# Talking-heads attention with two mixtures of experts: how the attention stage starts, loads and hands over

## The chip, the cores and the metric
One core of one Trainium2 chip runs the whole program. The metric is the time of the program on the device in microseconds (us). Three runs of the kernel before took 1065.91, 1069.70 and 1069.84 us; their median, 1069.7 us, is the time before.

## What is computed
All data is fp32. Attention has 4 batches, 12 heads, 448 positions and a head width of 64; its scores are mixed over the heads before the softmax and again after it ("talking heads"). Its result, 1792 rows of 768, goes through two layers of 8 experts with one expert per row:

```python
scores = einsum('bhij,hg->bgij', scale * q @ kT, w_pre)
attn   = softmax(scores, axis=-1)
attn   = einsum('bhij,hg->bgij', attn, w_post)
x      = (attn @ v) as 1792 x 768
# layer 1: e = argmax(cosine(x, expert_emb)); x = gate * relu(x @ w1[e]) @ w2[e]
# layer 2: only rows with x @ w_skip > 0:     x += gate * relu(x @ w1[e]) @ w2[e]
```

## The kernel before
**Attention** is cut into 16 units (u = 0 to 15; batch u // 4, a quarter m = u % 4 of its positions: 120 rows, or 88 for m = 3). The heads of a unit are taken in six pairs. `qk` (L310) computes the scores of one pair on TensorE; ScalarE, or for the first six pairs ScalarE and VectorE, copies them from PSUM to one of three `stage` buffers; `put` (L293) moves them by two DMAs on SyncE's queue into `sraw[u % 2]`, where heads and rows are interleaved on the 128 partitions, so that one matmul can mix the heads. A unit then has 6 steps (5 for m = 3). In a step `pre` (L334) mixes 120 rows, `top` and `ex` (VectorE, ScalarE) are the softmax, `post` (L378) mixes and turns the result with 128 small matmuls, and `out_t` copies it to `at`: one half by ScalarE (L406), one by VectorE (L408). The main loop (L1144) writes the order by hand: in step k it issues `pre(k + 2)`, `post(k)`, up to two `qk` pairs (a plan, L1140, gives "q" for a pair and "r" for a `rows_job`), and one `av` (L410), the product with v of the unit before. `av` writes the one PSUM bank with tag "D"; ScalarE alone empties it (L427), and it does so before the next `av` can begin.

What lies beside this main work waits in a list, `side`; `mu(n)` runs its next n entries, some ten a step. Among them is the routing of a finished unit: `rows_job` (L527) puts its rows back in order, writes them to `x_d` in DRAM (L588), finds each row's expert on VectorE (some 35 short operations one after the other), counts the row's place in that expert's list with a matmul (`rank`, L468) and scatters row number and gate to a table in DRAM (L490). `cum[1]` holds how many rows each expert has so far.

**The queues.** SyncE's queue carries the puts and, later, the expert weights. GpSimd's queue, which works strictly in order and has eight DMA semaphores in turn, carries q (`load_q`, three buffers), k (`load_k`, two buffers; k of a batch is one tile of 6 head pairs, loaded by two DMAs of 672 KB), v (`load_v`), the zeros and the tables.

**The start** (L1078 to L1107): q of unit 0 on SyncE's queue, k of batch 0 on ScalarE's queue in two parts, mixing weights and q on GpSimd's. Partitions 12, 25, 38, 51 and 77, 90, 103, 116 of `sraw` belong to no head, but `pre` multiplies them by zero weights, so they must hold finite numbers. Four DMAs on GpSimd's queue (L1092) copy zeros there, each to 4 partitions, 84 KB, before six `qk` pairs are run ahead.

**Other zeros.** `zero_fill` (L222) clears `y_d`, which the first layer scatters to: seven DMAs of 768 KB, one in step t = 3 of the units 1 to 7. Zeros also go to the last 89 rows of `x_d` (L217).

**The hand-over to the experts.** The first tile of 128 rows of expert 0 (`early`, L1116) is gathered from `x_d` by the table's first 128 places. It is closed by `pad_steps` (L605): a matmul counts the rows, and `cum[1]` is raised to 128 if there are fewer, so that later rows go to later places. This follows the routing of unit 14 (L546). At step `prefetch_at` (L1113; step t = 4 of unit 14), q, k and `stage` are given up for weights, and the first two of the weight chunks (128 x 1536 each) are loaded. Each chunk is split into a high and a low part: ScalarE rounds it (L723), and the rest is a subtraction (L728). `split_pieces` (L734) does this for the first four chunks in thirds, three thirds a step in the last unit, with the subtraction on GpSimd. After the loop (L1208 to L1217) the rest of `side` is run, and then the six `av` of unit 15; the buffers of attention are freed, the rows of unit 15 are computed (`rows_steps`, L551, L564), the first tile is turned (`t_T`, L775) and its first expert matmul follows (L781). The second tile of expert 0 needs the routing of unit 15: a read of the table (`entries`, 1024 entries), then a gather (L1238 and L1239).

Of the kernel before, what the change touches and what calls it, by code (L numbers as in the profile page):

```python
# [32 lines left out]
def talking_heads_moe_moe(tc, A, out):  # L33
# [177 lines left out]
    def setup_tables():  # L211
# [4 lines left out]
        st = [  # L216
            lambda: nc.gpsimd.dma_start(x_d[NTOK - 88:], z[:89]),  # L217
# [4 lines left out]
        fill = lambda r: nc.gpsimd.dma_start(yz[:, 2 * r:2 * r + 2], z.unsqueeze(1).to_broadcast([128, 2, DM]))  # L222
        return st, fill, z
# [54 lines left out]
    def load_k(b, lo=0, hi=6, eng=None):  # L278
        if lo == 0:
            ks[b] = aR.tile([128, 6, S], F32, tag="k", name="k", bufs=2)  # L280
        for g in range(2):
            (eng or nc.gpsimd).dma_start(
                ks[b][64 * g:64 * g + 64, lo:hi], A["kT"][b].rearrange("d (p g) j -> d g p j", g=2)[:, g, lo:hi]
            )
# [25 lines left out]
    def qk(u, pr, both=False, eng=None):  # L310
# [8 lines left out]
        for x in range(2):  # L319
            nc.tensor.matmul(p[x] if both else p[:, x], qs[u][64 * x:64 * x + 64, pr, :n], ks[b][64 * x:64 * x + 64, pr])  # L320
# [89 lines left out]
    def av(u, pr):  # L410
# [5 lines left out]
        p = psum("D", "av")[:, :10 * ng]  # L416
# [9 lines left out]
        def copy(o, i):  # L426
            nc.scalar.activation(o, i, AF.Copy)  # L427
# [99 lines left out]
    def rows_job(u, early):  # L527
# [8 lines left out]
        def evac():  # L536
# [9 lines left out]
            if u == NU - 2:  # L546
                side.extend([lazy(pad_steps), early])
# [57 lines left out]
    def pad_steps():  # L605
# [6 lines left out]
        def count():  # L612
            busy["D"] = True
            box["p"] = psum("D", "count")[:, :8]
            nc.tensor.matmul(box["p"], C["ones"], cum[1])
# [3 lines left out]
            lambda: free(v.tensor_scalar(pad[w], box["p"][w], -1.0, 128.0, op0=ALU.mult, op1=ALU.add)),  # L619
            lambda: v.tensor_scalar(pad[w], pad[w], 0.0, 1.0 / 32.0, op0=ALU.max, op1=ALU.mult),  # L620
            lambda: v.tensor_tensor(cum[1][w], cum[1][w], pad[w], op=ALU.add),
# [126 lines left out]
    def entry(tabi, row):  # L748
        ent = P["wL"].tile([128, 2], U32, tag="ent", name="ent", bufs=4)
# [327 lines left out]
    with ctx, tc.manual_schedule():  # L1077
        load_q(0, nc.sync)  # L1078
        load_k(0, 0, 2, nc.scalar)
        st, zero_fill, z = setup_tables()  # L1080
# [3 lines left out]
        ps["now"], ps["D"] = psA, 1  # L1084
        load_k(0, 2, 6, nc.scalar)
# [13 lines left out]
        load_q(2)  # L1099
# [26 lines left out]
        def pair():  # L1126
# [17 lines left out]
        for k in range(NT):  # L1144
# [3 lines left out]
            if u == 0:  # L1148
# [3 lines left out]
                if t == 3:  # L1152
                    load_q(3)
                if t == 5:
                    load_k(1)
            if u == NU - 1:
                plan = ("r" if t in (2, 3) else "", "")

            def job(x):
                if x == "q":  # L1160
                    pair()
                elif x == "r":
                    v = u - 2 if t == 2 else u - 1
# [22 lines left out]
            if u > 0:  # L1186
                n = 2 if u == NU - 1 else 1
# [10 lines left out]
                if t == 3 and u <= 7:  # L1198
# [6 lines left out]
            if k > prefetch_at:  # L1205
                for _ in range(3):
                    next(pieces, None)
        flush("dve")  # L1208
        flush("act")
        for f in state.pop("spare"):  # L1210
            f(psum("D", "rank"))
        while side:
            mu()
        last = rows_steps(NU - 1, 0)
        for p in range(6):
            av(NU - 1, p)
            flush("dve")  # L1217
# [190 lines left out]
```

## Time and profile before

| what | value |
|---|---|
| median of 3 runs | 1069.7 us |
| the profiled execution's own time | 1069.07 us |
| its span, first to last instruction | 1067.4 us |
| TensorE busy | 950.1 us, 89% of the span |
| VectorE busy | 685.1 us, 64% |
| ScalarE busy | 612.4 us, 57% |
| GpSimd busy | 316.8 us, 30% |
| DMA moved | 211.19 MB, 198 GB/s on average |
| mean granted clock of TensorE | 0.947 of full speed |

The span leaves 1.67 us of the execution's time outside it. A share of busy time is a mean over stages: up to some 500 us attention runs, then the first expert layer, then from some 850 us the second. PE is TensorE, PEld its weight loads, DVE VectorE, ACT ScalarE, POOL GpSimd, SPq SyncE's queue. "idle before <-X" names what ended the idle time ahead of an instruction; "issue" means that the profile shows no wait. L numbers are lines of the kernel.

### The profile page before, as it was taken

To read this page: it belongs to the slowest core of one execution; us is meant where nothing else is said; L and a number is where in the kernel's file an instruction comes from. 1 tells how busy PE (TensorE), PEld (TensorE's weight loads), DVE (VectorE), ACT (ScalarE), POOL (GpSimd) and SP (SyncE) were. 2 spreads that over 40 slices of the span, in tenths; PEclk is the share of its full clock that TensorE was granted. 3 is DMA by queue.
4 is the path that set the end of the run, shared out by engine and by line. 5 is a ranking of instruction groups with operands and counts; after the bars stand their busy time and mean duration, and the time that the engine had idled before them with its cause. 6 is when DMAs were issued, how large, how long until landed. Compare 5 with 4: busy or idle time off the path is not lost. (4 is left out here: it accounts for less than half of the span.)

```text
span 1067.4 us, 29848 instructions
## 1 busy us (share of the span) xinstructions
PE 950.1 (89%) x12292; PEld 752.3 (70%) x12292; DVE 685.1 (64%) x1897; ACT 612.4 (57%) x1123; POOL 316.8 (30%) x326
## 2 busy tenths in 40 slices
PE   3087979998999999985889999999999997999996
PEld 1034545565556655654679999999999986889895
DVE  1064646775677757765357666666666586889995
ACT  1064747775777778764355444444444455777773
POOL 5522201521142114024253123233232233153422
PEclk9588979998999999998689999999999998999999
DMA  8748446746564446333459866477566677899960
GB/s 113 152 129 213 115 147 169 189 146 188 160 170 112 128 137 145 108 118 115 150 222 409 315 207 207 164 237 228 176 220 209 203 261 267 307 366 385 379 233 15
DMA packets 67008, 211.19 MB, mean 198 GB/s; under 512 B 14580, under 2 KB 37745, under 8 KB 66864
## 3 DMA queue, kind: packets, MB, share of 16 engines
q1 hardware_dynamic: 44640, 139.85, 39.7%
q0 software_dynamic: 17184, 50.66, 18.2%
q10 hardware_dynamic: 5040, 18.69, 4.8%
q8 instruction: 99, 1.62, 0.7%
q14 instruction: 45, 0.37, 0.1%
HBM read 147.75 MB, written 28.57 MB: 165 GB/s over the span
## 5 line engine op out<-in xcount | busy, mean ns | idle before, releaser
L728 DVE TENSOR_TENSOR wl<-wraw,wh 128x1536 fp32r<-128x1536 f32 x146 | 254.6, 1761 | 8.0 <-ACT wh L723 8.0
L723 ACT ACTIVATE wh<-wraw 128x1536 fp32r<-128x1536 f32 (+1 forms) x160 | 224.4, 1420 | 18.5 <-PE y L783 5.3
L358 ACT ACTIVATE e<-pre,st 128x448 f32<-128x448 f32 x180 | 113.7, 633 | 81.2 <-DVE st L351 44.3
L420 PEld LDWEIGHTS av<-at,v 128*64 128x64 f32 x1536 | 80.9, 143 | 85.2 <-ACT xT L427 28.4
L391 PEld LDWEIGHTS post<-wp,e 60*64 60x64 f32 x5760 | 96.7, 137 | 55.3 <-issue 20.2
L320 PE MATMUL qk<-k,q 64*120 64x448 f32 (+1 forms) x384 | 105.0, 620 | 32.3 <-DVE stage L326 13.8
L350 DVE TENSOR_REDUCE st<-pre 128x1 f32<-128x448 f32 x180 | 110.8, 616 | 32.1 <-PE pre L340 31.0
L340 PE MATMUL pre<-sraw,wpre 64*64 64x448 f32 x720 | 103.9, 568 | 23.3 <-DMA q<-in_qU 16.9
L420 PE MATMUL av<-at,v 128*64 128x120 f32 (+1 forms) x1536 | 103.3, 277 | 22.3 <-ACT xT L427 17.6
L391 PE MATMUL post<-wp,e 60*64 60x60 f32 x5760 | 110.4, 224 | 8.0 <-issue 6.1
L328 ACT ACTIVATE stage<-qk 120x896 f32<-120x896 f32 (+1 forms) x90 | 83.8, 931 | 48.8 <-PE qk L320 42.4
L781 PE MATMUL h<-xh,wh 128*128 128x256 f32 x336 | 97.2, 289 | 0.0
L781 PE MATMUL y<-hh,wh 128*128 128x256 f32 x336 | 97.0, 289 | 0.0
L783 PE MATMUL h<-xh,wl 128*128 128x256 f32 x336 | 95.4, 284 | 1.0 <-DVE wl L728 1.0
L782 PE MATMUL h<-xl,wh 128*128 128x256 f32 x336 | 95.3, 284 | 0.0
L783 PE MATMUL y<-hh,wl 128*128 128x256 f32 x336 | 94.8, 282 | 0.0
L782 PE MATMUL y<-hl,wh 128*128 128x256 f32 x336 | 94.7, 282 | 0.0
L320 PEld LDWEIGHTS qk<-k,q 64*120 64x120 f32 (+1 forms) x384 | 29.4, 184 | 76.1 <-issue 31.7
L408 DVE COPY at<-post 128x480 f32<-128x480 f32 (+1 forms) x92 | 59.1, 642 | 30.9 <-PE post L391 30.8
L490 POOL DMA_INDIRECT tab<-c_ent,rt_dst x16 | 17.0, 1064 | 204.9 <-DVE rt_dst L485 200.2
L781 PE MATMUL y<-wh,hh 128*128 128x384 f32 x192 | 70.0, 365 | 0.0
L791 POOL DMA_INDIRECT out<-yr,ents x8 | 41.5, 5189 | 93.2 <-DVE yr L1045 93.2
(208 smaller groups left out, 2004.5 us busy)
## 6 DMA issues: line engine op xcount, KB each, us to landing
sraw<-stage SPq DMA_DIRECT2D x132, 210.0 KB
wraw<-in_w2a SPq DMA_DIRECT2D x36, 768.0 KB
wraw<-in_w2b SPq DMA_DIRECT2D x36, 768.0 KB
wraw<-in_w1a SPq DMA_DIRECT2D x30, 768.0 KB
wraw<-in_w1b SPq DMA_DIRECT2D x26, 768.0 KB
wraw<-in_w1b ACTq DMA_DIRECT2D x12, 768.0 KB
wraw<-in_w1a ACTq DMA_DIRECT2D x10, 768.0 KB
y_d<-zrow POOLq DMA_DIRECT2D x7, 768.0 KB, 7.2
```

The costliest lines, as they stand in the source:

```text
L320: nc.tensor.matmul(p[x] if both else p[:, x], qs[u][64 * x:64 * x + 64, pr, :n], ks[b][64 * x:64 * x + 64, pr])
L328: nc.scalar.activation(st[:n], p, AF.Copy)
L340: nc.tensor.matmul(p[r][64 * s:64 * s + 64], w[64 * r:64 * r + 64], sraw[u % 2][64 * r:64 * r + 64, slots_of(u, r) // 2 * s + t],)
L350: nc.vector.tensor_reduce(st[:, r:r + 1], p[r], op=ALU.max, axis=AX.X, negate=True)
L358: nc.scalar.activation(e[r], p[r], AF.Sigmoid, bias=st[:, r:r + 1], accum_out=st[:, 2 + r:3 + r])
L391: nc.tensor.matmul(p[s][64 * hf:64 * hf + 64, c, r], e[r][64 * s:64 * s + HB, j:j + 64], w[64 * s:64 * s + HB, r],)
L420: nc.tensor.matmul(p[64 * s:64 * s + 64].rearrange("p (s g i) -> p s g i", s=2, i=5), v[:, c, 64 * s:64 * s + 64], a[:, :, c, :ng, 5 * g:5 ...
L723: nc.scalar.activation(wt[key, c][0][:, a:b], wraw[key, c][:, a:b], AF.Copy)
L728: eng.tensor_tensor(lo[:, a:b], wraw[key, c][:, a:b], hi[:, a:b].bitcast(F32), op=ALU.subtract)
L781: nc.tensor.matmul(p, a[0], b[0], start=start, stop=False)
L782: nc.tensor.matmul(p, a[0], b[1], start=False, stop=False)
L783: nc.tensor.matmul(p, a[1], b[0], start=False, stop=stop)
```

## The change
1. VectorE sets both `sraw` tiles whole (128 x 5376 each) to zero by a memset at the start; the four DMAs of L1092 go.
2. k of a batch becomes three tiles of two head pairs, each loaded by two DMAs of 224 KB: for batch 0 on ScalarE's queue, for batch 1 in steps 1, 3, 5 of unit 0, for batches 2 and 3 each part as soon as its old buffer was read. `load_q(2)` moves from behind the first six pairs to step 1 of unit 0, `load_q(3)` from step 3 to step 4.
3. `zero_fill` writes 384 KB, in step 1 of the units 1 to 14.
4. The low part of the first four weight chunks is subtracted by VectorE. One third a step (and four more `side` entries) instead of three, starting after step 2 of unit 14; what is left is done after `side`.
5. Unit 14 also runs two `av` a step, and the rows of the units 12 and 13 are routed earlier; the first tile is closed after unit 12, not 14, and for expert 0 alone; its count uses spare PSUM columns. Two more DMAs zero rows 1464 to 1703 of `x_d` (360 KB each).
6. After the loop the six `av` of unit 15 come before the rest of `side`, in three PSUM banks (tag "P"), emptied by ScalarE and VectorE in turn; then `side`, then the weight thirds that are left. The turn of the first tile comes before the rows of unit 15. The second tile reads 128 table entries of its own and is gathered before the lists of all experts are read.

```diff
-        fill = lambda r: nc.gpsimd.dma_start(yz[:, 2 * r:2 * r + 2], z.unsqueeze(1).to_broadcast([128, 2, DM]))
+        fill = lambda r: nc.gpsimd.dma_start(yz[:, r], z)
...
+            *(lambda o=o: nc.gpsimd.dma_start(x_d[NTOK - o:NTOK - o + 120], z[:120]) for o in (328, 208)),
...
-    def load_k(b, lo=0, hi=6, eng=None):
-        if lo == 0:
-            ks[b] = aR.tile([128, 6, S], F32, tag="k", name="k", bufs=2)
+    def load_k(b, j, eng=None):
+
+        t = ks[b, j] = aR.tile([128, 2, S], F32, tag=f"k{j}", name="k", bufs=2)
...
-    def av(u, pr):
+    def av(u, pr, tag="D", eng=None):
...
-            if u == NU - 2:
+            if u == NU - 4:
                 side.extend([lazy(pad_steps), early])
...
-        def count():
-            busy["D"] = True
-            box["p"] = psum("D", "count")[:, :8]
-            nc.tensor.matmul(box["p"], C["ones"], cum[1])
+        def count(p=None):
+            if p is None:
+                state["spare"].append(count)
+                side.insert(0, wait)
+                return
+            box["p"] = p[:, :1]
+            nc.tensor.matmul(box["p"], C["ones"], cum[1][:, 0:1])
...
-                lo_part(a, a + 512, nc.gpsimd)
+                lo_part(a, a + 512, nc.vector)
...
+        for i in range(2):
+            sraw[i] = aL.tile([128, 12, S], F32, name=f"sraw{i}")
+            nc.vector.memset(sraw[i], 0.0)
...
-        for i in range(2):
-            sraw[i] = aL.tile([128, 12, S], F32, name=f"sraw{i}")
-            for o in (12, 77):
-                nc.gpsimd.dma_start(sraw[i][o:o + 40:13], z[:4, :S].unsqueeze(1).to_broadcast([4, 12, S]))
...
-        load_q(2)
...
-        prefetch_at = first[15] - 2
+        prefetch_at = first[14] + 2
...
-            box["ents", 0] = entries(1, 0)
-            box["f00"] = gather(x_d, box["ents", 0][:, 0], "wR", 1)
+            box["f00"] = gather(x_d, entry(1, 0, rt), "wR", 1)
...
-                if w % 4 == 3 and w // 4 + 2 < B:
-                    load_k(w // 4 + 2)
+            if pr % 2 and w % 4 == 3 and w // 4 + 2 < B:
+                load_k(w // 4 + 2, pr // 2)
...
-                if t == 3:
-                    load_q(3)
-                if t == 5:
-                    load_k(1)
-            if u == NU - 1:
-                plan = ("r" if t in (2, 3) else "", "")
+                if t in (1, 4):
+                    load_q(2 + t // 4)
+                load_k(1, t // 2) if t % 2 else None
+            if u >= NU - 2:
+                plan = ("q" if u < NU - 1 and t < 2 else "r" if t == 3 else "", "r" if u < NU - 1 and t == 0 else "")
...
-                n = 2 if u == NU - 1 else 1
+                n = 2 if u >= NU - 2 else 1
...
-                if t == 3 and u <= 7:
+                if t == 1 and u <= 14:
                     zero_fill(u - 1)
...
-                for _ in range(3):
-                    next(pieces, None)
+                next(pieces, None)
+                mu(4)
...
+        for p in range(6):
+            av(NU - 1, p, "P", (None, nc.vector)[p % 2])
+            flush("dve")
         while side:
             mu()
+        for _ in pieces:
+            pass
         last = rows_steps(NU - 1, 0)
-        for p in range(6):
-            av(NU - 1, p)
-            flush("dve")
...
-        todo = last[:8] + t_T(t, xg) + last[8:]
+        todo = t_T(t, xg) + last
...
-            box["ents", 1] = entries(1, 1)
-            box["f01"] = gather(x_d, box["ents", 1][:, 0])
+            box["f01"] = gather(x_d, entry(1, 128))
+            for s in range(2):
+                box["ents", s] = entries(1, s)
             m1_gather(1)
```

## Rows read from the trace of the kernel before

**Rows 1.** The page: TensorE's busy tenths in 40 slices; a costliest group.
```profile
PE   3087979998999999985889999999999997999996
...
L728 DVE TENSOR_TENSOR wl<-wraw,wh 128x1536 fp32r<-128x1536 f32 x146 | 254.6, 1761 | 8.0 <-ACT wh L723 8.0
```

**Rows 2.** Waits, 0 to 60 us: who for whom, total us, times, longest.
```profile
ACT stage L325 <- DMA sraw<-stage: 22.9, 3, 15.9
```

**Rows 3.** Timeline, 0 to 76 us: start, us, engine line op out<-in xcount [idle before].
```profile
12.80 27.37 SPq L304 DMA_DIRECT2D sraw<-stage  x9
...
43.83 0.78 SPq L307 DMA_DIRECT2D sraw<-stage  x1
...
52.86 3.21 PE L340 MATMUL pre<-sraw,wpre 64*64 64x448 f32 x10 [16.85 <-DMA q<-in_qU]
...
61.46 14.22 SPq L304 DMA_DIRECT2D sraw<-stage  x12
```

**Rows 4.** DMA issues, 0 to 60 us: KB each, median us to landing.
```profile
sraw<-zrow POOLq DMA_DIRECT2D x4, 84.0 KB, 15.2
q<-in_qU POOLq DMA_DIRECT2D x2, 162.0 KB, 4.1
```

**Rows 5.** Groups by line, 0 to 25 us: memsets, busy us and mean ns.
```profile
L215 POOL MEMSET zrow<- 128x768 f32 x1 | 0.7, 737 | 0.3 <-POOLq L1397 0.3
...
L110 DVE MEMSET wpre<- 128x64 f32 x1 | 0.1, 112 | 0.0
```

**Rows 6.** Windows, one unit each (2, 3, 6, 10, 11, 15): PE, PEld, DVE, ACT, POOL busy.
```profile
121.57:158.78 37.21, 30.88 (x576) 17.80 (x568) 19.13 (x75) 19.98 (x48) 6.66 (x9) 0.82 0.56 154
158.78:183.39 24.61, 22.50 (x460) 13.96 (x460) 15.09 (x58) 17.40 (x41) 4.24 (x6) 1.00 0.60 166
236.37:268.89 32.52, 29.70 (x576) 17.09 (x568) 19.20 (x75) 19.80 (x47) 6.62 (x9) 0.90 0.62 172
345.75:371.66 25.91, 25.86 (x576) 15.95 (x568) 19.03 (x75) 19.69 (x47) 4.54 (x6) 1.00 0.45 132
371.66:396.30 24.64, 22.53 (x460) 13.95 (x460) 15.12 (x58) 17.39 (x41) 3.49 (x5) 1.00 0.48 134
473.86:499.63 25.77, 17.25 (x340) 13.77 (x340) 11.68 (x34) 14.57 (x34) 14.98 (x13) 0.87 0.37 111
```

**Rows 7.** Waits in unit 2, 121.57 to 158.78 us.
```profile
POOL q L273 <- PE qk L320: 21.3, 1, 21.3
...
PE pre L340 <- DMA sraw<-stage: 3.0, 2, 2.6
```

**Rows 8.** DMA issues in unit 2, 121.57 to 158.78 us.
```profile
k<-in_kT POOLq DMA_DIRECT2D x2, 672.0 KB, 12.7
y_d<-zrow POOLq DMA_DIRECT2D x1, 768.0 KB, 15.3
```

**Rows 9.** Groups by line in unit 15, 473.86 to 499.63 us.
```profile
L728 POOL TENSOR_TENSOR wl<-wraw,wh 128x512 fp32r<-128x512 f32 x12 | 15.0, 1276 | 9.6 <-ACT wh L723 9.6
L420 PE MATMUL av<-at,v 128*64 128x120 f32 x80 | 5.8, 290 | 8.0 <-ACT xT L427 8.0
...
L372 DVE TENSOR_TENSOR wp<-wpost,st 128x120 f32<-128x120 f32 (+1 forms) x3 | 2.5, 849 | 0.1
```

**Rows 10.** Timeline, 498 to 548 us: from the last post to the second tile.
```profile
498.52 1.08 PE L391 MATMUL post<-wp,e 60*64 60x60 f32 x32 [0.69 <-ACT at L406]
...
508.61 1.47 PE L420 MATMUL av<-at,v 128*64 128x90 f32 x16 [0.36 <-DVE rt_pad L619]
...
520.63 3.02 PE L564 MATMUL rows<-r,xT 128*88 128x136 f32 x12
...
524.13 0.93 PE L775 MATMUL xTp<-c_consts,xg 128*128 128x128 f32 x6 [0.48 <-DMA xg<-x_d,ents]
...
525.31 0.50 PE L781 MATMUL h<-wh,xh 128*128 128x512 f32 x1 [0.26 <-ACT xh L776]
...
546.64 0.50 PEld L775 LDWEIGHTS xTp<-c_consts,xg 128*128 128x128 f32 x3 [5.46 <-issue]
```

More of the change, by code (lines that the diff above doesn't have):

```diff
@@ L221, in setup_tables @@
             st.append(lambda i=i: nc.gpsimd.dma_start(tab[i].rearrange("(p r) c -> p (r c)", p=128), A["sentinel"]))
-        fill = lambda r: nc.gpsimd.dma_start(yz[:, 2 * r:2 * r + 2], z.unsqueeze(1).to_broadcast([128, 2, DM]))
-        return st, fill, z
+        fill = lambda r: nc.gpsimd.dma_start(yz[:, r], z)
+        return st, fill
     def pieces_of(m):
@@ L319, in qk @@
         for x in range(2):
-            nc.tensor.matmul(p[x] if both else p[:, x], qs[u][64 * x:64 * x + 64, pr, :n], ks[b][64 * x:64 * x + 64, pr])
+            nc.tensor.matmul(p[x] if both else p[:, x], qs[u][64 * x:64 * x + 64, pr, :n], ks[b, pr // 2][64 * x:64 * x + 64, pr % 2])
         def evac():
@@ L415, in av @@
             xT[u] = aL.tile([128, 6, UR], F32, tag="xT", name="xT", bufs=2)
-        p = psum("D", "av")[:, :10 * ng]
+        p = psum(tag, "av")[:, :10 * ng]
         for c in range(4):
@@ L426, in copy @@
         def copy(o, i):
-            nc.scalar.activation(o, i, AF.Copy)
+            if eng is None:
+                nc.scalar.activation(o, i, AF.Copy)
+            else:
+                eng.tensor_copy(o, i)
         def evac():
@@ L610, in pad_steps, with wait @@
         w = slice(96, 128)
-        def count():
-            busy["D"] = True
-            box["p"] = psum("D", "count")[:, :8]
-            nc.tensor.matmul(box["p"], C["ones"], cum[1])
+        def count(p=None):
[5 more added lines that the diff above has]
+            nc.tensor.matmul(box["p"], C["ones"], cum[1][:, 0:1])
+        def wait():
+            if "p" not in box:
+                side.insert(0, wait)
         return [
             count,
-            lambda: free(v.tensor_scalar(pad[w], box["p"][w], -1.0, 128.0, op0=ALU.mult, op1=ALU.add)),
-            lambda: v.tensor_scalar(pad[w], pad[w], 0.0, 1.0 / 32.0, op0=ALU.max, op1=ALU.mult),
-            lambda: v.tensor_tensor(cum[1][w], cum[1][w], pad[w], op=ALU.add),
+            lambda: v.tensor_scalar(pad[w, 0:1], box["p"][w], -1.0, 128.0, op0=ALU.mult, op1=ALU.add),
+            lambda: v.tensor_scalar(pad[w, 0:1], pad[w, 0:1], 0.0, 1.0 / 32.0, op0=ALU.max, op1=ALU.mult),
+            lambda: v.tensor_tensor(cum[1][w, 0:1], cum[1][w, 0:1], pad[w, 0:1], op=ALU.add),
         ]
@@ L745, in split_lo, with entry @@
             lo_part(0, 1536, eng or nc.vector)
-    def entry(tabi, row):
-        ent = P["wL"].tile([128, 2], U32, tag="ent", name="ent", bufs=4)
+    def entry(tabi, row, pool=None):
+        ent = (pool or P["wL"]).tile([128, 2], U32, tag="ent", name="ent", bufs=4)
         nc.gpsimd.dma_start(ent, tab[tabi][row:row + 128] if isinstance(row, int) else tab[tabi][bass.ds(row, 128)])
@@ L1078, in talking_heads_moe_moe @@
         load_q(0, nc.sync)
-        load_k(0, 0, 2, nc.scalar)
-        st, zero_fill, z = setup_tables()
+        load_k(0, 0, nc.scalar)
+        st, zero_fill = setup_tables()
         warm = const.tile([1, 2], F32, name="warm")
@@ L1162, in job @@
                 elif x == "r":
-                    v = u - 2 if t == 2 else u - 1
+                    v = u - 2 if t != 3 else u - 1
                     if v >= 0:
```

5 lines of the change are left out of this document (3 added, 2 removed).

## The prediction, made before the changed kernel was run
> **What bounds the kernel now.** I read the page first. TensorE is busy 89% of the span, so a gain must come from where it is not: its 40 slices show holes in the first two, again at the fourth, the sixth and the tenth, and from the eighteenth to the twenty-first [rows 1]. From slice 22 on TensorE is the bound and the change touches nothing there. So I read three places one by one.
>
> The start, next, in the waits and the timeline. ScalarE stood 22.9 us for puts to free a `stage` buffer [rows 2]. SyncE issued nine puts over 27.4 us from 12.80 on, the last one at 43.83, and the first `pre` ran at 52.86, 9.0 us behind it; unit 0, with no zeroing beside it, issued twelve puts in 14.22 us [rows 3]. The zero DMAs of L1092 move only 84 KB each and take 15.2 us to land, where 162 KB of q take 4.1 [rows 4]: they write to four partitions each, and the puts queue behind them.
>
> Then the units, by windows. Units 2, 6 and 10 are of one kind and take 37.21, 32.52 and 25.91 us; 2 and 6 load a k, 10 does not. Units 3 and 11 are of one kind too, 24.61 and 24.64, the first with a `y_d` fill and the second without [rows 6]. In unit 2 TensorE waits for puts [rows 7], while 1344 KB of k and a fill of 768 KB take 12.7 and 15.3 us to land [rows 8].
>
> Last, the end of attention. Unit 15 takes 25.77 us without a single `qk` [rows 6]: GpSimd subtracts for 15.0 us, three short VectorE operations at L372 take 849 ns on average, and TensorE's `av` waits 8.0 us for ScalarE [rows 9]. From the end of the last `post` (499.60) to the first expert matmul (525.31) there are 25.7 us: 9.0 of routing, 12.0 of six `av` in one PSUM bank, then the rows of unit 15 and the turn [rows 10].
>
> **The start.** The zeros now cost two memsets of 5376 columns. The nearest row in length is GpSimd's 768 columns in 737 ns, 0.96 ns a column; VectorE's 64 columns in 112 ns make 1.75 [rows 5]. That bounds the pair between 10.3 and 18.8 us. I take 10.3: VectorE's fixed part hardly counts in so long an instruction. From about 1 us on it ends at 11.3, before the first put at 12.80, so it costs nothing; at the other end it costs 7.
>
> Puts then run from 12.80 as in unit 0: thirteen at 14.22/12 = 1.19 us, so the last is issued at 28.2. Landing takes 4.1 (the quick q load) to 9.0 us (the last put of before), hence the first `pre` at 32.3 to 37.2. I take 36, since constants and v are loaded beside it as before: 17 us earlier. Against that, what GpSimd's queue loaded while TensorE stood now comes beside unit 0's steps, with 720 KB more zeros for `x_d`. Unit 2 paid 11.3 us for 2112 KB [rows 6, 8], 0.53 us per 100 KB; so 720 KB cost up to 3.8 us, and as much again if the moved loads hurt as well, or nothing if they fit between puts. I take 2. Start: **-15**, between -20 and -8.
>
> No row shows a long VectorE memset beside GpSimd's DMA issues. At worst the mixing weights' DMAs slip by the whole 10.3 us and VectorE's copies with them, at best by nothing; I take nothing, since GpSimd issued its DMAs in 0.74 us each (6.66/9) in unit 2, where VectorE was busy half the time [rows 6]. The Trainium skill (SBUF — State Buffer, "Who interferes with whom") agrees with that choice for an instruction with at most one SBUF input outside VectorE's two-port modes. The same page's box on VectorE blocking GpSimd's descriptors would describe the other outcome; by it, as an estimate, the start would give about 5 and the sum would be 1040. No row here decides between the two.
>
> **k and fills in parts.** The excess of units 2 and 6 over unit 10 is 11.3 + 6.6 = 17.9 us. At the step where a whole k met a fill there is now a third of k and half a fill, 832 of 2112 KB. If the stall goes with the bytes, 39% stays and 10.9 us go; if only what exceeds the slack of the puts counts, all 17.9 go; if the two earlier thirds merely stall units 1 and 5 instead, only the halved fill helps, 18% or 3.3. The seven new fills in units 8 to 14 cost nothing while a fill of 768 KB costs unit 3 nothing beside unit 11. I take **-12**, from -18 to -3.
>
> More DMAs are issued: 12 for k, 7 fills, 2 for `x_d` and 1 list less 4 zeroings on GpSimd's queue, so 18 at 0.74 us, 13 us over fifteen units. They lie beside its wait for TensorE (21.3 us in unit 2 [rows 7]); without that cover they would push x_d and table writes, which nothing reads before the first tile's list. Two more on ScalarE's queue fall before its first copy. `load_q(2)` moves past the constants and two v loads on GpSimd's queue and is needed only in unit 0's step 3; `load_q(3)` waits for the same `qk` as before, with the k thirds now ahead of it.
>
> **Units 14 and 15.** ScalarE rounds one third a step instead of three, and VectorE takes over the subtraction at a third of 1761 ns [rows 1], 0.6 us a step, without GpSimd beside it. TensorE's 8.0 us of waiting should fall by some two thirds, 5 us. Unit 14 has its `av` two a step, the second waiting for ScalarE to empty the one bank: +1. Together **-4**; the best is 25.77 - 17.25 = 8.5 (unit 15 without any TensorE idle), the worst +3 if unit 14 pays that wait three times over.
>
> **The hand-over.** After the last `post`: 1 us until its result is copied, six `av` at 1.47 = 8.8 with no wait between them, 0.5 to empty the last (12.0/6 - 1.47), about 3 for the end of the routing and the last four weight thirds on VectorE (4 x 0.6 and a few short steps; 0 to 5), 0.9 for the turn, 3.0 for the rows, 0.3: 17.5 against 25.7, **-8**, from -12 to -5. The second tile starts 26.0 us after unit 15's rows (520.63 to 546.64 [rows 10]); these now start 14.2 instead of 21.0 us after the last `post`, 7 us sooner, and its list is shorter, 1 us: the gain of 8 is kept through that stall. Closing the first tile sooner is worth 0.5 us by itself, TensorE's wait for it [rows 10]; it is the cover for the rest, since a gather only 0.5 us ahead of TensorE would eat most of the 8. Its own wait stands on GpSimd's queue: the `x_d` writes of units 13 to 15 queue behind the gather, with a step or more of slack each. Late next, where these stalls go, are unit 0's loads and unit 15's routing.
>
> **Sum.** -15 - 12 - 4 - 8 = -39, against the profiled execution's own 1069.07 us: **1030 us**. That execution stands 0.6 us below the median, so no correction. A measurement of this kernel can tell about 0.5% (5 us) from no change.
>
> **The rivals.** *The start stays starved* (0.15): GpSimd's queue, no longer held up by the zeroing, pours q, v and k out beside the first puts, and `pre` begins near 48 instead of 36. For it: puts landed only 9.0 us after issue with v beside them [rows 3]. Against: in that time the queue issues many small pieces first. The start gives 3: 1042.
>
> *The hand-over is a chain* (0.13): the second tile waits for unit 15's routing, now with six weight chunks streaming beside its scatter, list and gather; the first tile only arrives earlier to wait longer, and the last two terms give 2 instead of 12: 1040. For it: the wait of 5.46 us is there already [rows 10].
>
> *Slower: parts that starve puts* (0.06). Six k parts and fourteen fills make twenty meetings with the puts on GpSimd's queue. If each held TensorE as long as unit 2's puts did, 3.0 us [rows 7], they would cost 60 us in place of 17.9; with 27 gained elsewhere that is +15: 1084. It turns slower from (27 + 17.9)/20 = 2.2 us a meeting. Against: unit 3 [rows 6]. The Trainium skill (DMA: Bandwidth & Descriptors, "Rules for kernel authors") speaks for this side: it wants a MiB or more in a DMA for bandwidth, and that page's "Anatomy of one DMA" puts a fixed 2.0 us on each. By it the 18 more would be an estimated 36 us if nothing hid them, and the sum 1078. The trace does not bear that out so far, as 84 KB took longer than 162 KB [rows 4].
>
> *Everything at its best end* (0.08): -20 - 18 - 8.5 - 12: about 1010.
>
> **How the numbers follow.** The forecast keeps 0.58. The range 1012 to 1052 holds it, the first two rivals, and nearly both at once (1052); it leaves out the slower rival and most of the best case. Faster by over 0.5%: 0.58 + 0.15 + 0.13 + 0.08, less 0.02 for rivals that meet, 0.92; within 0.5%: 0.02; slower: 0.06.
>
> **What would show it.** Right: the first `pre` between 32 and 38 us, two memsets near 5 us before 13 us, units 2 and 6 under 30 us, no subtraction on GpSimd in unit 15, the first expert matmul about 17 us after the last `post`. Wrong: a `pre` near 50, TensorE waiting for puts in units 1 and 5 or in each unit from 8 on, a memset of 9 us or more, or over 8 us of wait for the second tile.

## The result, and the profile after the change

The changed kernel took **1042.25 us** (median of four runs, 1038.77 to 1045.34) against 1069.77 us: a ratio of **0.975, 95% interval 0.9703 to 0.9797**. Forecast were 1030 us and a range of 1012 to 1052. The profiled execution took 1039.31 us, its span 1037.7 (1067.4 before).

Slices of the changed kernel, from its page (compare [rows 1]):

```profile
PE   3479899999999999767789999999999999999996
...
L739 DVE TENSOR_TENSOR wl<-wraw,wh 128x1536 fp32r<-128x1536 f32 (+1 forms) x158 | 262.7, 1681 | 9.3 <-ACT wh L734 8.5
```

The second row is the costliest group, VectorE's weight subtraction: 158 of them now, for 146 in [rows 1]. The holes of the first two slices are smaller, those of the fourth, sixth and tenth nearly gone. But slices 17 to 21 now read 7 6 7 7 8, where 18 to 21 read 8 5 8 8: the end of attention begins to suffer one slice sooner. Stage by stage, the two traces differ as follows. A unit is taken here, and in all windows of this document, from ScalarE's first copy of its `post` result (`at`) to the same copy of the next unit.

| stage | before, us | after, us | difference | forecast |
|---|---|---|---|---|
| start of unit 1 | 94.38 | 82.05 | -12.3 | -15 |
| units 1 to 13 | 354.14 | 342.13 | -12.0 | -12 |
| unit 14, then unit 15 to the end of the last `post` | 51.08 | 59.81 | **+8.7** | -4 |
| last `post` to the second tile | 47.07 | 38.04 | -9.0 | -8 |
| second tile to the end | 520.8 | 515.7 | -5.1 | 0 |

The split between the first two rows depends on that mark. Before the change, ScalarE's first copy of unit 1 came 5.0 us after the first `post` matmul (89.37 to 94.38), mostly because ScalarE stood waiting for a put (2.7 us); after it, 1.4 us. Taken from the first `post` matmul of a unit, the first row is -8.7 and the second -15.6. Their sum, -24.3, is the same either way.

**The start.** Timeline of the changed kernel, 0 to 48 us (start, duration; compare [rows 3]):

```profile
2.13 4.54 DVE L1098 MEMSET sraw<- 128x5376 f32 x1 [1.10 <-issue]
7.74 4.54 DVE L1098 MEMSET sraw<- 128x5376 f32 x1 [1.07 <-issue]
12.51 17.27 SPq L305 DMA_DIRECT2D sraw<-stage  x12
29.83 0.77 SPq L308 DMA_DIRECT2D sraw<-stage  x1
38.22 3.21 PE L341 MATMUL pre<-sraw,wpre 64*64 64x448 f32 x10 [16.62 <-DMA sraw<-stage]
```

The memsets end at 12.28, ahead of the first put at 12.51. Thirteen puts go out by 29.83 us instead of 43.83, and the first `pre` runs at 38.22 instead of 52.86. ScalarE's wait for puts ahead of the first `pre` fell from 22.9 us [rows 2] to 10.3.

**The units.** Windows of one unit each after the change: 2, 6, 10, 11, 14 and 15 (columns as in [rows 6]: window and its length, busy time of PE, PEld, DVE, ACT, POOL with counts, granted clock, DMA share, GB/s):

```profile
108.94:135.83 26.89, 25.37 (x552) 15.17 (x552) 17.33 (x72) 19.48 (x48) 6.39 (x9) 1.00 0.57 166
...
214.07:244.59 30.52, 28.02 (x560) 16.63 (x556) 18.08 (x74) 19.73 (x49) 6.32 (x9) 0.89 0.52 150
321.45:347.36 25.91, 25.86 (x576) 15.95 (x568) 19.04 (x75) 19.70 (x48) 5.13 (x7) 1.00 0.50 147
347.36:372.02 24.66, 22.55 (x460) 13.97 (x460) 15.11 (x58) 17.38 (x41) 4.06 (x6) 1.00 0.51 150
424.18:460.92 36.74, 27.23 (x582) 19.43 (x576) 21.18 (x83) 19.95 (x48) 3.04 (x4) 0.91 0.27 90
460.92:484.04 23.12, 14.85 (x340) 11.06 (x336) 13.63 (x55) 11.62 (x31) 4.01 (x4) 0.93 0.26 74
```

Units 2 and 6 fell from 37.21 and 32.52 to 26.89 and 30.52. Unit 11 now has a fill beside it and stands at 24.66 (24.64 without). Unit 14 takes 36.74 us, and TensorE is idle in it for 9.5 us. Before the change it was this:

```profile
448.52:473.86 25.34, 23.79 (x572) 15.69 (x564) 19.55 (x76) 17.07 (x45) 2.67 (x3) 1.00 0.36 115
```

TensorE's waits for `av` (us in total, times, longest), in unit 14 and then in unit 15 of the changed kernel, and the first of them in the timeline:

```profile
PE av L421 <- ACT xT L429: 7.4, 3, 2.7
...
PE av L421 <- ACT xT L429: 6.9, 3, 4.1
```
```profile
426.21 1.05 PE L421 MATMUL av<-at,v 128*64 128x120 f32 x16
...
427.20 0.84 ACT L593 ACTIVATE sq<-xd 120x768 f32<-120x768 f32 x1
...
428.20 0.64 ACT L359 ACTIVATE e<-pre,st 128x448 f32<-128x448 f32 x1
...
428.92 0.64 ACT L359 ACTIVATE e<-pre,st 128x448 f32<-128x448 f32 x1
...
429.55 0.37 ACT L429 ACTIVATE xT<-av 128x120 f32<-128x120 f32 x1
...
429.96 1.07 PE L421 MATMUL av<-at,v 128*64 128x120 f32 x16 [2.70 <-ACT xT L429]
```

The first `av` ends at 427.26. The copy that empties its bank takes 0.37 us, but stands behind two `e` in ScalarE's order (here also behind `sq`, a step of unit 12's routing), so the second `av` starts 2.70 us late. Three steps of unit 14 and three of unit 15 do the same, each with two `e` ahead of the copy. In the longest wait, 4.1 us, ScalarE itself is idle for 2.0 us ahead of the first `e`, which waits for VectorE and its routing.

**The hand-over**, timeline 484 to 523 us (compare [rows 10]):

```profile
486.25 5.62 PE L421 MATMUL av<-at,v 128*64 128x90 f32 x96 [2.27 <-DVE rt_lg L604]
...
492.24 0.88 PE L786 MATMUL xTp<-c_consts,xg 128*128 128x128 f32 x6
492.95 1.55 PE L568 MATMUL rows<-r,xT 128*88 128x136 f32 x12
493.06 3.09 DVE L739 TENSOR_TENSOR wl<-wraw,wh 128x512 fp32r<-128x512 f32 x5
...
494.29 0.50 PE L792 MATMUL h<-wh,xh 128*128 128x512 f32 x1
...
496.67 0.50 PE L794 MATMUL h<-wh,xl 128*128 128x512 f32 x1 [1.65 <-DVE xl L788]
```

From the end of the last `post` (483.99) to the first expert matmul there are 10.3 us, where there were 25.7. Six `av` take 5.6 us in one run; the unit's rows take 1.55 us, where [rows 10] has 3.02. The second tile follows 38.0 us after the last `post` (47.1 before). TensorE waits for its gather longer than the 5.2 us of before:

```profile
PE xTp L786 <- DMA xg<-x_d,ent: 7.0, 1, 7.0
```

### The profile page after: what moved, and what is told of

Same layout as the page of the kernel before. It is cut to its first block, busy times and chain, and to the rows that moved or that the text cites. A ratio compares the mean times of both kernels' runs of the same rounds, so it can differ in the third digit from the quotient of the medians.

```text
span 1037.7 us, 29871 instructions
## 1 busy us (share of the span) xinstructions
PE 939.2 (91%) x12292; PEld 748.7 (72%) x12292; DVE 699.8 (67%) x1920; ACT 610.8 (59%) x1114; POOL 310.7 (30%) x333
## 5 line engine op out<-in xcount | busy, mean ns | idle before, releaser
L739 DVE TENSOR_TENSOR wl<-wraw,wh 128x1536 fp32r<-128x1536 f32 (+1 forms) x158 | 262.7, 1681 | 9.3 <-ACT wh L734 8.5
L421 PEld LDWEIGHTS av<-at,v 128*64 128x64 f32 x1536 | 77.9, 139 | 81.9 <-ACT xT L429 27.4
L392 PEld LDWEIGHTS post<-wp,e 60*64 60x64 f32 x5760 | 97.8, 139 | 52.4 <-issue 13.7
L351 DVE TENSOR_REDUCE st<-pre 128x1 f32<-128x448 f32 x180 | 111.0, 616 | 27.5 <-PE pre L341 26.6
L321 PE MATMUL qk<-k,q 64*120 64x448 f32 (+1 forms) x384 | 102.6, 611 | 25.7 <-ACT stage L329 12.0
L421 PE MATMUL av<-at,v 128*64 128x120 f32 (+1 forms) x1536 | 98.3, 270 | 22.6 <-ACT xT L429 20.4
L494 POOL DMA_INDIRECT tab<-rt_ent,rt_dst x17 | 26.5, 1560 | 142.7 <-DVE rt_dst L527 96.9
```

The lines of the kernel that those rows point to most:

```text
L351: nc.vector.tensor_reduce(st[:, r:r + 1], p[r], op=ALU.max, axis=AX.X, negate=True)
L392: nc.tensor.matmul(p[s][64 * hf:64 * hf + 64, c, r], e[r][64 * s:64 * s + HB, j:j + 64], w[64 * s:64 * s + HB, r],)
L421: nc.tensor.matmul(p[64 * s:64 * s + 64].rearrange("p (s g i) -> p s g i", s=2, i=5), v[:, c, 64 * s:64 * s + 64], a[:, :, c, :ng, 5 * g:5 ...
L739: eng.tensor_tensor(lo[:, a:b], wraw[key, c][:, a:b], hi[:, a:b].bitcast(F32), op=ALU.subtract)
```

## The experiments

The runs are on several chips, and on two of them even undisturbed units are longer (last section). So the stall of units 2 and 6 is taken as their excess over unit 10 of the same trace, and the time of a whole kernel is relied on only where both kernels ran several times on one chip. Experiments 1 to 5, 9, 11 and 12 have one run each.

**1. Zeroing by VectorE alone**, in the kernel before. The memsets stand ahead of the second part of k.

```
-            for o in (12, 77):
-                nc.gpsimd.dma_start(sraw[i][o:o + 40:13], z[:4, :S]...)
+            nc.vector.memset(sraw[i], 0.0)
```

> The kernel before with one part of the change: the four zeroing DMAs are gone and VectorE zeroes the two score buffers; loads, fills and the end of attention stay as before. Theory (the zeroing DMAs held the first puts back, and what is left is the puts' latency beside the loads): first pre near 38 us as in the changed kernel (52.86 before), unit 0 as long as before (32.7 us), unit 1 starts near 80, the whole 1069 - 14 = 1055 us. Rival (the loads in smaller parts and their new order were needed as well): first pre at 44 us or later, the whole above 1061.

Measured: the first `pre`

```profile
40.25 3.22 PE L340 MATMUL pre<-sraw,wpre 64*64 64x448 f32 x10 [16.55 <-DMA sraw<-stage]
```

and unit 1 at 84.17, -10.2 of the changed kernel's -12.3. The kernel of experiment 3, on the same chip and with the start of before, has them at 55.08 and 96.13, so that on one chip the gain is 14.8 and 12.0 us. The zeroing DMAs were what held the start. What the loads add can't be read from the 2.0 us that `pre` still lacks: in nine traces with the whole change `pre` comes between 35.9 and 39.1.

The whole missed the 1055 us expected: 1068.59 beside 1072.74, one run each. In this trace the units 1 to 13 take 362.6 us for the 354.1 of before, nearly all of them longer; and the stretch after attention, which experiments 1 to 3 don't touch, took 567, 572 and 561 us in them. So single runs on this chip can't show a gain of 10 us in the whole.

**2 and 3. k in thirds alone; fills halved and spread alone**, each in the kernel before.

```
+        t = ks[b, j] = aR.tile([128, 2, S], F32, tag=f"k{j}", name="k", bufs=2)
...
-        fill = lambda r: nc.gpsimd.dma_start(yz[:, 2 * r:2 * r + 2], ...)
+        fill = lambda r: nc.gpsimd.dma_start(yz[:, r], z)
...
-                if t == 3 and u <= 7:
+                if t == 1 and u <= 14:
```

> The kernel before with k alone in thirds, issued two pairs apart; fills stay 768 KB each in units 1 to 7. Theory (the stall of units 2 and 6 is k and a fill meeting in one step, and goes with the bytes of the meeting): unit 2 falls from 37.2 to about 30 us, unit 6 from 32.5 to about 31, the whole about 1069 - 8 = 1061. Rival 1 (k is all of it): unit 2 at 27, unit 6 at 30, 1057. Rival 2 (the fill is what holds the puts up): unit 2 above 34, the whole above 1065.

> The kernel before with the fills alone halved and spread over units 1 to 14, two steps earlier in each unit; k stays whole (1344 KB in one step). Theory: unit 2 falls from 37.2 to about 33 us (the fill no longer stands in the step of k, k itself still does), unit 6 from 32.5 to about 31, the whole about 1069 - 5 = 1064; units 8 to 14 unchanged within 0.3 us each. Rival 1 (the fill is what holds the puts up): unit 2 at 27 to 28, 1058. Rival 2 (the fill plays no part): unit 2 at 36 or more, 1068 to 1070.

Excess of units 2 and 6 over unit 10, with the kernels told further down:

| kernel | unit 2 | unit 6 | sum, us |
|---|---|---|---|
| before | 11.30 | 6.61 | 17.9 |
| zeroing alone | 10.18 | 6.20 | 16.4 |
| k in thirds alone | 5.49 | 3.87 | 9.4 |
| fills alone | 9.59 | 9.46 | 19.1 |
| changed kernel | 0.98 | 4.61 | 5.6 |
| changed kernel again | 2.94 | 5.04 | 8.0 |
| no fills in units 1 to 7 (experiment 10) | 0.00 | 1.31 | 1.3 |

Windows of units 2, 6 and 10 with k in thirds, then with the fills alone:

```profile
118.81:150.97 32.16, 28.16 (x548) 16.60 (x552) 16.97 (x70) 19.76 (x48) 6.54 (x9) 0.89 0.52 154
233.00:263.54 30.54, 28.15 (x569) 17.11 (x568) 18.82 (x74) 20.13 (x49) 6.53 (x9) 0.94 0.54 163
342.86:369.53 26.67, 26.22 (x573) 16.29 (x569) 19.00 (x74) 19.80 (x48) 4.54 (x6) 1.00 0.44 128
```
```profile
124.19:160.41 36.22, 30.40 (x572) 17.92 (x568) 18.99 (x74) 20.02 (x48) 6.47 (x9) 0.86 0.56 147
239.75:275.84 36.09, 30.76 (x573) 17.75 (x568) 19.18 (x74) 20.09 (x48) 6.42 (x9) 0.86 0.56 144
355.32:381.95 26.63, 26.18 (x573) 16.29 (x569) 19.00 (x74) 19.81 (x47) 5.15 (x7) 1.00 0.48 142
```

k in thirds is worth 8.5 of the 17.9 us (7.0 against the zeroing kernel, on the same chip). The fills alone are worth nothing: beside a whole k, even halved and two steps away, unit 2 keeps 9.6 us of excess and unit 6 has 2.9 us more, a miss of the theory for which no run has the cause. With k in parts the fill does seem to count: 9.4 us are left with the whole fill, 4.6 to 8.0 in the nine traces of kernels that have both parts of the change, and 1.3 without a fill beside k. Each of these is one trace, and two traces of the same kernel differ by 2.4.

The whole took 1074.52 and 1076.08 us beside the same 1072.74, not the 1061 and 1064 expected; as above, these single runs decide nothing.

**4. One `av` a step in unit 14 again**, in the changed kernel.

```
-                n = 2 if u >= NU - 2 else 1
+                n = 2 if u == NU - 1 else 1
```
The rows of unit 13 move back to unit 15.

> The changed kernel with unit 14 taking one av a step again, as all units before it; the rows of unit 13 move back to unit 15's third step. All else stays as changed. Theory (unit 14's 36.7 us come from the second av of a step, which waits for ScalarE to empty the one bank behind the two e of the step): unit 14 back to 26 us, unit 15 near 25, last post near 484 - 9 = 475, the whole about 1039 - 9 = 1030. Rival (unit 14 is long because routing and weight rounding were moved into it): unit 14 stays above 33 us and the whole within 3 us of 1039.

```profile
434.51:461.70 27.19, 25.42 (x563) 15.83 (x556) 20.44 (x79) 17.23 (x46) 3.03 (x4) 1.00 0.35 120
461.70:483.12 21.42, 14.89 (x356) 11.63 (x352) 12.15 (x44) 12.17 (x29) 1.96 (x2) 1.00 0.22 75
```

These windows are its units 14 and 15, the second to the end of the last `post`: 11.2 us less together. Since unit 13's rows moved as well, this run alone doesn't separate the doubled `av` from the routing; experiment 7 does. The whole took 1040.63 us (kernel before on this chip: 1079.12), not the 1030 of the theory. One reason is the chip: units 1 to 13 took 355.4 us here, for 342.1 in the trace of the changed kernel. The other can be read in the trace. With unit 13's rows in unit 15, routing is left over: TensorE waits 6.4 us for `rt_oh` after the last `post` (its longest wait 4.9), the first expert matmul comes 16.6 and the second tile 42.1 us after it. Some 4 to 6 us of the gain are given back there.

**5. VectorE empties the first `av` of a step**, in the changed kernel.

```
-                    av(u - 1, p)
+                    av(u - 1, p, "D", nc.vector if n == 2 and p % 2 == 0 else None)
```

> The changed kernel, with VectorE instead of ScalarE emptying the first av of each step in units 14 and 15 (the second stays ScalarE's). Theory (the wait is for ScalarE's place in its order, not for the bank as such): the second av follows the first by about 1.5 us instead of up to 4, units 14 and 15 fall from 36.7 and 23.1 to about 28 and 19 us, the whole to about 1039 - 12 = 1027. Rival 1 (VectorE has no room there: its routing, maxima and weight subtractions queue behind): the gap moves to VectorE's next operation and less than 4 us go. Rival 2 (the work itself is doubled in the step and TensorE's order costs it): units 14 and 15 change by less than 2 us.

Waits of TensorE in its unit 14:

```profile
PE av L421 <- DVE rt_lg L135: 2.2, 1, 2.2
PE av L421 <- DVE rt_m L500: 2.1, 1, 2.1
PE av L421 <- DVE xT L431: 1.1, 1, 1.1
```

Unit 14 stayed at 36.13 us and only unit 15 gained 2.0 (the whole: 1046.09, for 1027 by the theory): rival 1. VectorE's copy stands behind two maxima and the routing's short steps as ScalarE's stood behind two `e`. Whichever of the two empties it, the bank waits for that engine's order.

**6 and 7. A second bank for the second `av`, beside the changed kernel unaltered**, on one chip.

```
-                    av(u - 1, p)
+                    av(u - 1, p, "PD"[p % 2] if n == 2 else "D")
```

> The changed kernel once more, unaltered, as the reference on the chip on which the next two run. 1039 to 1046 us; unit 14 near 36.5 us, first expert matmul 10.3 us after the last post, second tile 38 us after it.

> The changed kernel, with the first av of a step in units 14 and 15 in a bank of the three that hold pre, the second in the one av bank; ScalarE empties both. Theory (two av a step cost their wait for one bank; with VectorE as the emptier the wait went to VectorE's routing queue, 2 us each again): no av waits for the other, unit 14 falls from 36.7 to about 27 us, unit 15 from 23.1 to about 20, the hand-over keeps its 10.3 us, the whole 10 to 13 us below the unaltered changed kernel. Rival 1 (pre then waits for its bank, which the xT copy holds): unit 14 at 32 us or more, 0 to 5 us gained. Rival 2 (ScalarE itself is the bound of these steps): steps 0 to 2 of unit 14 stay above 6 us each.

Unaltered: 1043.38 us, 0.9739 of before (0.9699 to 0.9779). With two banks: **1026.15 us, 0.9587 (0.9555 to 0.962)**, six runs each. Its units 14 and 15, and the whole of TensorE's waits for `av` in unit 14:

```profile
422.03:451.88 29.85, 25.35 (x576) 17.19 (x570) 21.00 (x83) 18.86 (x49) 3.03 (x4) 1.00 0.34 111
451.88:468.23 16.35, 14.34 (x346) 10.84 (x342) 13.29 (x55) 10.86 (x31) 4.01 (x4) 1.00 0.36 105
```
```profile
PE av L421 <- ACT e L359: 0.5, 1, 0.5
```

46.2 us for the two, where the unaltered trace beside it has 59.9 (36.74 and 23.14) and the kernel before 51.1. The granted clock stays at 1.00 instead of 0.91 and 0.93. The hand-over keeps its 10.2 us. The edit changes nothing but the bank, so the one bank cost 13.7 us here. Without that cost, all that the change does in the two units (doubled `av`, less rounding, VectorE's subtraction) is worth 4.9 us; no run separates these three. The medians are 17.2 us apart, more than the 10 to 13 expected: in the two traces, units that the edit doesn't touch and the start are 4.6 us shorter too.

**8. Two banks, and two weight thirds a step**, so that none is left at the turn.

```
-                next(pieces, None)
+                for _ in range(2):
+                    next(pieces, None)
```

> As the two-bank kernel, and from the third step of unit 14 on two thirds of a weight chunk are rounded and subtracted a step instead of one, so that none is left behind the last av. Theory (the five subtractions of 0.6 us that VectorE has left stand ahead of the first tile's xl and of unit 15's routing): the third expert matmul follows the second at once instead of 1.6 us late, and the second tile comes 2 to 3 us sooner after the last post (36 instead of 38); the whole 2 us below the two-bank kernel. Rival (VectorE and ScalarE pay the same 0.6 us a step earlier, on the path of units 14 and 15): units 14 and 15 grow by as much, no difference within 1 us.

The second tile came 31.9 us after the last `post`, 6 us sooner, but units 14 and 15 grew from 46.2 to 52.7: the rival, and at more than its price. VectorE's subtractions there went from five, 3.4 us, to eleven, 7.6 us. The whole was 1034.61 us, 8 worse than with two banks alone, on the same chip; as the profiled execution is only 4 us longer, part of that isn't placed.

**9. The last six `av` in one bank, emptied by ScalarE**, in the changed kernel.

```
-            av(NU - 1, p, "P", (None, nc.vector)[p % 2])
+            av(NU - 1, p)
```

> The changed kernel, with the last six av (unit 15's) in the one bank D again and emptied by ScalarE alone, as before; still ahead of the rest of the routing. Theory (the two banks and engines are worth the six av's waits, 12.0 against 5.6 us): first expert matmul 6 us later after the last post (16 instead of 10.3 us), and second tile 4 to 6 us later since its list waits for unit 15's rows; the whole about 1039 + 5 = 1044. Rival (the order alone, av ahead of the routing, is what brought the gain): first expert matmul within 2 us of 10.3, the whole within 2 us of 1039.

From the last `post` to the first expert matmul, first in the changed kernel, then in this one (windows; the clock is the third number from the end):

```profile
483.99:494.30 10.31, 8.05 (x119) 7.90 (x119) 7.08 (x36) 5.22 (x19) 0.85 (x1) 0.83 0.34 104
```
```profile
495.72:515.40 19.68, 13.48 (x118) 11.87 (x119) 7.81 (x30) 7.33 (x28) 2.37 (x3) 0.51 0.22 64
```

9.4 us more to the first expert matmul and 7.1 more to the second tile (45.2), the theory and more; the whole 1057.19 for the 1044 expected. The five waits between the `av` sum to only 3.3 us. Most of the rest is TensorE's own work, which takes 13.5 us for 8.1 at a clock of 0.51 for 0.83, so nearly all of it at the lower of the two levels. The whole time is not all due to the edit: this chip, too, has the longer units (units 1 to 13: 354.1 us), and unit 14, ahead of the edit, took 39.5.

**10. Fills only from unit 8 on; weight thirds behind unit 15's rows**, on the two-bank kernel.

```
-                if t == 1 and u <= 14:
-                    zero_fill(u - 1)
+                if t in (1, 3) and 8 <= u <= 14:
+                    zero_fill(2 * (u - 8) + t // 2)
...
-        for _ in pieces:
-            pass
...
-        todo = t_T(t, xg) + last
-        load_w(2, nc.gpsimd)
+        todo = t_T(t, xg) + last[:8] + [leftover] + last[8:]
```
`leftover` does the weight thirds that are left, then `load_w(2, nc.gpsimd)`.

> The two-bank kernel with two more edits, read each in its own stage. (1) No fill in units 1 to 7; two fills of 384 KB in each of units 8 to 14. Theory (what is left of the stall in units 2 and 6 goes with the bytes that meet, 448 KB of k with 384 KB of fill): unit 2 from 27.8 to about 26.5 us, unit 6 from 29.8 to about 28, units 8 to 14 unchanged within 0.3 us. Rival (k, q and v are enough by themselves): units 2 and 6 unchanged within 0.5 us. (2) The weight thirds left after attention are rounded and subtracted after the first tile's xl and after unit 15's rows are emptied, not ahead of them, and two weight chunks are loaded after that. Theory (VectorE's 3.1 us of subtraction stand on the path to the third expert matmul and to unit 15's routing): the third expert matmul at once behind the second (1.6 us of wait gone), the second tile about 35.5 instead of 37.9 us after the last post. Rival (the weights then come late): the first tile waits for wh or wl and the second tile is no sooner. Together about 1021 to 1023 us by theory, 1026 by the rivals.

**1019.44 us, 0.9558 (0.9519 to 0.9596)**, the lowest time of all; but it ran on another chip than the two-bank kernel, and the intervals of the two ratios overlap, so the gain is read by stages. Both theories held there. Units 2 and 6 came to 25.90 and 27.21, while units 8 to 14, with two fills each, stayed within 0.4 us of the two-bank kernel, but for unit 8, which had been 0.6 us longer there. The second tile came 34.4 us after the last `post` and no longer waits for its gather. TensorE's waits up to it are now

```profile
PE rank L480 <- DVE rt_oh L468: 3.3, 1, 3.3
PE hTp L964 <- ACT hr L952: 2.3, 1, 2.3
PE av L421 <- DVE rt_lg L604: 2.3, 1, 2.3
```

the first of which is unit 15's routing itself, behind the 3.1 us of subtractions. That is what stands in the way next.

**11. The first tile closed after unit 14's rows**, as before, in the changed kernel.

```
-            if u == NU - 4:
+            if u == NU - 2:
```

> The changed kernel with the first expert's first tile closed as late as before: after the rows of unit 14 in place of those of unit 12; its padding count is taken when attention's matmuls are through. Forecast's reading (closing sooner was the cover for the earlier turn): the tile's x arrives some 12 us after TensorE is ready for it, so that the first expert matmul comes 20 to 25 instead of 10.3 us after the last post; but the second tile, which waits for unit 15 anyway, stays at 38 to 40 us after it, so the whole loses only 0 to 4 us. Rival 1 (the cover decides): both tiles shift by 8 us or more, 1050 or above. Rival 2 (no cover needed): the first expert matmul stays within 2 us of 10.3.

```profile
PE xTp L788 <- DMA xg<-x_d,ent: 20.0, 2, 15.0
```

TensorE waits 15.0 us for the first tile and 5.0 for the second. The first expert matmul comes 28.4 us after the last `post`, the second tile 50.2 (47.1 before the change); the whole 1057.21. Rival 1: the second tile is 12.2 us later, not 0 to 2. Without the early closing the other edits of the hand-over gain nothing by the second tile.

**12. The last `av` behind the routing again**, in the changed kernel: `while side: mu()` ahead of the six `av`.

> The changed kernel with the last six av behind the rest of unit 14's routing again, as before; the two banks, the two emptying engines and the early closing stay as changed. Theory (the routing no longer shares VectorE with GpSimd's subtractions, so little of it is left when the last post ends): av starts about 2 us later than in the changed kernel, first expert matmul about 12 instead of 10.3 us after the last post, second tile 38 to 40 instead of 38.0; the whole within 3 us of the changed kernel. Rival (the order is what took the 9.0 us of routing away that stood between the last post and the first av before): av starts 7 to 9 us after the last post instead of 2.3, first expert matmul at 16 us or later, second tile 43 or later, the whole 5 us or more slower.

```profile
485.35 0.57 PE L480 MATMUL rank<-rt_oh,c_consts 120*120 120x8 f32 x2 [3.50 <-DVE rt_oh L468]
486.25 6.03 PE L421 MATMUL av<-at,v 128*64 128x90 f32 x96
```

First expert matmul 12.9 us after the last `post` (10.3), second tile 36.2 (38.0; the theory had 38 to 40), the whole 1043.66 in one run: the order itself is worth about nothing, as the theory had it, and the rival's 43 us or later is refuted.

## Why the prediction was right, and where it was off

The time lies in the range, but not because each term came out. One term failed, the hand-over came near by another sum, and 5.1 us that were not forecast helped. The measured 1042 us is also the number of the first two rivals, for neither's reason.

**The start** (-15, measured -12.3, or -8.7 by the first `post`) was right in its mechanism: the zeroing alone makes most of the gain (experiment 1). The zeroing took 9.1 us, under the lower bound of 10.3 from GpSimd's row, and hid in front of the first put. The last put went out at 29.83 (28.2 forecast) and the first `pre` followed 8.4 us later, at 38.2 for the 36 I took. Unit 0 was 1.5 us longer than before, for the 2 I took; that agreement shows little, since unit 0 varies from 30.3 to 34.2 us in the ten traces with the memsets. The starved start fell: `pre` came at 36 to 40 us in every kernel with the memsets. The mixing weights were not held up: GpSimd issued their DMAs in 0.50 us each beside the memsets as before, and VectorE waited 0.65 us for them. So what the Trainium skill's box on VectorE blocking GpSimd's descriptors describes (SBUF — State Buffer, "SBUF: two separate sides") did not happen here.

**k and fills** (-12, measured -12.0, or -15.6 by the first `post`): a stall that goes with the bytes that meet was to leave 7.0 of the 17.9 us; 5.6 and 8.0 were left in the two traces of the changed kernel. That the first number agrees to the tenth is luck. The same rule would leave 10.3 us with k alone in thirds (1216 of 2112 KB; 9.4 measured) and 3.8 without the fill (448 KB; 1.3 measured), but it fails for the fills alone, which should have taken some of the stall and took none. So the size is near, and the rule itself is not shown. The alternative that the halved fill alone would help, 3.3 us, is refuted: it gave none. That twenty meetings each cost 2.2 us or more is refuted too: units 8 to 13, each with a fill, are within 0.1 us of before. Nor did 18 more DMAs cost the 36 us estimated from the Trainium skill (DMA: Bandwidth & Descriptors, "Anatomy of one DMA"). GpSimd had room for them: its waits that end in unit 2 are still 18.0 us for the routing and 8.0 for `qk`.

**Units 14 and 15** (-4, measured +8.7): this is the step that failed. "The second waiting for ScalarE to empty the one bank: +1", with +3 as the worst. No row stands behind that price, and it makes the wait 1 us at a time; the copy itself takes 0.37 us. But the wait lasts until the copy's turn comes in ScalarE's order, behind two `e`: up to 2.7 us in unit 14 and 4.1 in unit 15, three times in each, 14.3 us in all. A second bank alone takes 13.7 us out of the two units (experiment 7). The same error stands in unit 15. I put the 8.0 us of [rows 9] down to ScalarE being filled by weight rounding and expected two thirds of it to go; with five thirds of a chunk rounded there instead of ten, 6.9 us stayed, and a second bank took them all. What I expected of the subtraction did come, in unit 15 of the changed kernel (groups by line: count, busy us, mean ns):

```profile
L739 DVE TENSOR_TENSOR wl<-wraw,wh 128x512 fp32r<-128x512 f32 x3 | 2.0, 683 | 0.0
...
L373 DVE TENSOR_TENSOR wp<-wpost,st 128x120 f32<-128x120 f32 (+1 forms) x4 | 1.1, 267 | 0.1
```

A third costs VectorE 0.68 us, and the short operation beside it 267 ns instead of 849. Without the bank's wait the two units give -4.9, near the number I had.

**The hand-over** (-8, measured -9.0 at the second tile) came near, but by another sum. The first expert matmul came 15.4 us sooner, not 8, because I took the durations of [rows 10], which were at about half the clock (this stretch before the change, granted clock 0.54):

```profile
499.60:525.31 25.71, 15.22 (x124) 12.77 (x124) 7.55 (x49) 6.16 (x28) 6.64 (x8) 0.54 0.48 150
```

In the changed kernel, at 0.83, the `av` cost 0.94 us each, not 1.47, and the rows 1.55, not 3.0, and the rest of the routing lay beside them. The second tile did not keep all of that: its wait grew to 7.0 us, with five subtractions ahead of unit 15's routing (without any left there, it came 6 us sooner in experiment 8). So the rival *the hand-over is a chain* named the right wait, though it took 6.4 us of the gain and not all. That closing the tile sooner is the cover for the rest was right, and worth more than I gave it, 12.2 us.

**The rest**: 5.1 us after the second tile come from no step of mine. Other kernels with the change spent 514 to 524 us there, so they lie within what changes from trace to trace. Terms and rest sum to the measured -29.7; 1030 was 9.3 us short of the profiled execution because of 12.7 us in units 14 and 15, less 3.4 for the other errors together.

Of the prediction's own signs, the memsets, the wait for the second tile (7.0, under 8) and GpSimd's subtractions came as said. Two missed narrowly, the first `pre` (38.2 for 32 to 38 us) and unit 6 (30.5 for under 30), and the first expert matmul came 10.3 us after the last `post`, not 17.

## What to carry to other kernels

Price a wait for a buffer by the place of the releasing instruction in its engine's order, not by its duration: two uses of one bank in a step cost up to 4.1 us where the copy took 0.37, moving the copy to another engine changed little, and a second bank freed it. A duration read next to a stall may carry a lowered clock; look at the granted clock before using it in a sum. Read a stage's stall as the excess over an undisturbed unit of the same trace, since runs and chips can differ by more than the effect. And say by which instruction a stage begins: another mark moved 3.6 us from one stage to the next here.

## What was not expected of the hardware

In the six kernels of experiments 1 to 5 and 9, which ran on two chips, units that nothing disturbs were 0.4 to 1.1 us longer than on the three chips of the other experiments (unit 10: 26.6 to 26.7 for 25.9). The extra stands inside `post`: a run of its matmuls in the zeroing kernel, ahead of unit 9,

```profile
312.05 1.33 PE L391 MATMUL post<-wp,e 60*64 60x60 f32 x50
313.75 0.45 PE L391 MATMUL post<-wp,e 60*64 60x60 f32 x12 [0.37 <-issue]
```

is broken by a pause in which TensorE waits for nothing that the profile shows; the same 64 matmuls ran unbroken in 1.16 us in the kernel before, and take 2.2 here. In units 8 to 13 there are six or seven such pauses on those two chips, 2.5 to 3.0 us of waiting in all, and none to two in the other kernels. The runs that they break are about 1 us longer each, 6.2 to 7.5 us together, and the six units take 160.3 to 160.7 us for 154.8 to 156.4. Why is open; as each of these kernels ran on one chip alone, the chip is the likely cause but not the shown one.

A memset of 5376 columns took VectorE 4.54 us, 0.84 ns a column. In the changed kernel the list's reading goes out 7.4 us after the scatter of unit 15's entries (503.53 to 510.89 us), with the weights streaming beside it. Whether the weights are the cause is not shown.
